# Unit 0 of a fused convolution and MLP: diagonal taps on turned blocks in place of band matmuls, and what goes with it

## The chip, the cores and the metric

One core of one Trainium2 chip. The time is that of one execution of the program on the device, in microseconds (us); the number that counts is the median of several runs. All times below are in us unless marked otherwise.

## The reference

`x` is (8, 4096, 192) in fp32, `weight` (8 heads, 7 taps), `w_in` (192, 2048), `w_out` (2048, 192). A causal convolution along the sequence with softmaxed taps, one set of taps for each group of 24 channels, is followed by a two-layer MLP:

```python
w = softmax(weight, axis=-1)                       # 8 x 7
out[b, s, h, g] = sum_k w[h, k] * x_pad[b, s + k, h, g]   # x_pad: 6 zero rows ahead of the sequence
h = out.reshape(32768, 192) @ w_in
y = (h * cos(h)) @ w_out                           # 32768 x 192, fp32
```

## The kernel before

**Tiles and units.** The 32768 tokens are cut into 64 tiles of 512 tokens; two tiles are a unit of 1024 tokens, eight blocks of 128. Each tile runs *product 1* (`mm1`, L488, matmul on L503): for each of 8 pairs of 128 hidden columns, h0 to h7, six matmuls with 64 contraction rows each, two of them side by side on the two halves of the PE array, write one `h` tile in PSUM, 128 x 1024 fp32. `gcu` (L506) then lets ACT write `cs = sin(h + pi/2)` (L510) and DVE `g = h * cs` (L514). *Product 2* (`mm2_step`, L523, matmul on L552) sums 64 steps of two matmuls into two PSUM banks `o_ps0` and `o_ps1`; `evac` (L567) copies them out and `store` writes them. `h` tiles come from a pool of three; the same pool serves the convolutions of later units, so a new tile waits until an old one has been read.

**Convolution of a unit.** `conv_part` (units 1 to 3) and `conv_unit` (from 4) multiply blocks of x, cast to bf16 on POOL (`cast_unit`, L207), with band matrices `band` (128 x 8 x 256) that hold the taps on diagonals; the result is copied by ACT to `ct`, doubled, and turned into channel-major form `cT` by a transposing DMA (`turn_unit`, L309). Product 1 reads `cT`.

**The start, which the change rebuilds.** `weight` is fetched as 4 rows of 14 numbers (L81). x of unit 0 is fetched in two halves: four blocks at once (L114), four more only after the SP queue has waited for `diag` (L406, L407); behind them stand unit 1 (L408 to L410) and, after another wait, `w_out` (L441 to L443). `w_in` is fetched in bf16 by two DMAs on POOL's queue (L111, L112, called on L165), behind the building of two small masks on POOL. PE runs 3 and 9 matmuls on zeros (`keep_warm`, L134) around one that spreads the taps over the partitions (L150); softmax of the taps in six small operations on DVE and ACT (L175 to L185); `prod` and `diag` (L401, L404) turn them into pieces of the band, which DVE, POOL and ACT copy to `band` in 16 pieces (L412 to L416). `conv_first` (L427) convolves four blocks with 32 matmuls of 48 columns, ACT and DVE copy them doubled to `ct` (L438), `turn_first` (L445) turns them with 12 matmuls against `ident` into PSUM, and ACT and DVE copy those to `cT` (L457). The other four blocks of unit 0 are convolved within tile 0 (`conv_rest`, L459, token `r`) and turned by a DMA (token `X0`).

**Order.** The schedule is manual: each engine does its instructions in the order in which the program writes them. For each tile two strings give that order. In the PE string `h3` is product 1 of pair 3 (`h0a`, `h0b` its halves), `m11` eleven steps of product 2, `d11`/`c11` the two band groups of unit 1, `w5` five matmuls on zeros, `W0`/`W1` POOL's cast of a half of `w_out`, `K1` POOL's cast of unit 1, `L2` the load of unit 2. In the ACT string `s3` is `gcu` of pair 3 and `er`, `ed11` copies of a convolution. For the first tile:

```python
PE_FIRST[0]  = "K1 h0a h0b W0 h1 h2 h3 r h4 w5 d11 w4 h5 d21 W1 c11 X0 m1 h6 m11 h7 L2 c21 D1"
ACT_FIRST[0] = "s0a s0b s1 s2 er s3 s4 ed11 ed21 s5 ec11 s6 ec21 s7"
```

Of the kernel before, what the change touches and what calls it, by code (L numbers as in the profile page):

```python
# [16 lines left out]
def kernel(  # L17
# [40 lines left out]

    xf = x.rearrange("b s d -> (b s) d")
# [20 lines left out]
    w_row = consts.tile([4, HQ * K], FP32)  # L80
    nc.scalar.dma_start(out=w_row, in_=weight.rearrange("(q h) k -> q (h k)", q=4))  # L81
# [25 lines left out]
    w = consts.tile([128, NC, NP, 128], BF16)  # L107
    w_src = moe_w_in.rearrange("(m k) (t f) -> t m k f", k=NC, t=2)
    HP = NP // 2
# [4 lines left out]
    load_unit(0, 0, NB)  # L114
# [12 lines left out]

    one = consts.tile([128, 1], FP32)
    nc.vector.memset(one, 1.0)
    zero = consts.tile([128, T], BF16)  # L130
    nc.vector.memset(zero, 0.0)  # L131
    idle = o_pools[0].tile([128, T], FP32, name="o_ps0")

    def keep_warm(n, bank=idle):  # L134
        for _ in range(n):
# [3 lines left out]
    quarter = consts.tile([4, 128], FP32)  # L139
    nc.gpsimd.memset(quarter, 1.0)  # L140
    nc.gpsimd.affine_select(out=quarter, in_=quarter, compare_op=ALU.is_ge, fill=0.0, base=0, pattern=[[1, 128]],
                            channel_multiplier=-32)
    nc.gpsimd.affine_select(out=quarter, in_=quarter, compare_op=ALU.is_ge, fill=0.0, base=31, pattern=[[-1, 128]],
                            channel_multiplier=32)
# [4 lines left out]
    w_bc = w_all[:, 0 : HQ * K].rearrange("p (h k) -> p h k", k=K)  # L149
    nc.tensor.matmul(out=w_all[:, 0 : HQ * K], lhsT=quarter, rhs=w_row, start=True, stop=True)  # L150
    keep_warm(9)


    xb0 = consts.tile([128, UB + 1, D], BF16, name="x_bf0")

    E = 32 + K - 1
    mask = consts.tile([128, E, K], BF16)
    nc.gpsimd.memset(mask[0:32], 0.0)
    nc.gpsimd.affine_select(out=mask[0:32], in_=mask[0:32], compare_op=ALU.not_equal, fill=1.0, base=1 - K,  # L159
                            pattern=[[1, E], [1, K]], channel_multiplier=-1)  # L160
    band = consts.tile([128, H, 256], BF16)
    nc.vector.memset(band, 0.0)
    for q, copy in enumerate((nc.vector.tensor_copy, nc.scalar.copy, nc.scalar.copy)):
        copy(out=mask[32 * q + 32 : 32 * q + 64], in_=mask[0:32])  # L164
    for t in range(2):  # L165
        load_w(t)
    nc.gpsimd.memset(xb0[:, 0, :], 0.0)
    ident = consts.tile([128, 128], BF16)
    nc.gpsimd.memset(ident, 0.0)
    nc.gpsimd.affine_select(out=ident, in_=ident, compare_op=ALU.not_equal, fill=1.0, base=0, pattern=[[1, 128]],  # L170
                            channel_multiplier=-1)
    wn = consts.tile([128, HQ, K], BF16)
    ct_bufs = [consts.tile([128, 2 * NC * NPB + 1, 64], BF16, name="ct_buf%d" % i) for i in range(2)]

    wmax = consts.tile([128, HQ, 1], FP32)  # L175
    nc.vector.tensor_reduce(out=wmax[:, :, 0], in_=w_bc, axis=mybir.AxisListType.X, op=ALU.max)
    wexp = consts.tile([128, HQ, K], FP32)
    nc.vector.tensor_tensor(out=wexp, in0=w_bc, in1=wmax.to_broadcast([128, HQ, K]), op=ALU.subtract)
    nc.scalar.activation(out=wexp, in_=wexp, func=AF.Exp)
    nc.scalar.activation(out=scrap, in_=one, func=AF.Sin)  # L180
    wsum = consts.tile([128, HQ, 1], FP32)
    nc.vector.tensor_reduce(out=wsum[:, :, 0], in_=wexp, axis=mybir.AxisListType.X, op=ALU.add)
    winv = consts.tile([128, HQ, 1], FP32)
    nc.vector.reciprocal(winv, wsum)
    nc.vector.tensor_tensor(out=wn, in0=wexp, in1=winv.to_broadcast([128, HQ, K]), op=ALU.mult)  # L185
    wo = consts.tile([128, NP, 2, D], BF16)
# [291 lines left out]

    conv_first()
    turn_first(0)  # L480
    turn_first(1)

# [241 lines left out]
```

## Time and profile before

| | |
|---|---|
| median of 3 runs | 705.23 (705.06 to 705.26) |
| the profiled execution | 705.18, its span 703.5 |
| busy over the span | PE 697.0, ACT 644.4, DVE 642.4, POOL 503.7 |
| the groups with most busy time | L514 DVE `g` 604.9, L510 ACT `cs` 511.0, L552 PE 420.6, L503 PE 407.0 |
| DMA | 100.09 MB, mean 142 GB/s |

How to read the profile: busy time is the time in which an engine runs an instruction. A row of a timeline gives start, duration, engine, line, operation, `out<-in` by the program's names, count, and in square brackets the idle time just before and what ended it. A row of a group gives busy time and mean length (ns) in place of the start. The chain of waits goes back from the last instruction, at each step to what released it. Matmul durations in a timeline hold some 0.17 of pipeline; neighbours in it start closer together than they are long. Times count from the start of the span; the kernel's first instruction on each engine stands at 0.8 to 0.9.

### The profile page before, as it was taken

How to read it: one execution, taken by the hardware profiler on the slowest of the kernel's cores; microseconds unless marked ns; L12 is line 12 of the kernel's file. 1: busy time of each engine (PE TensorE's matmuls, PEld its weight loads, DVE VectorE, ACT ScalarE, POOL GpSimd, SP SyncE). 2: the span in 40 equal slices, each digit the busy share in tenths (PEclk: the TensorE clock that was granted, in tenths of full speed). 3: DMA queues.
4: the chain of work that ended last, by engine and by line, in shares of the span. 5: the costliest groups of instructions: out<-in, count | busy, mean ns of one | idle time of the engine just before them, and what ended most of it. 6: DMA issues, size and time to landing. Idle time of an engine off the chain costs nothing.

```text
span 703.5 us, 26826 instructions
## 1 busy us (share of the span) xinstructions
PE 697.0 (99%) x11830; PEld 512.8 (73%) x11830; DVE 642.4 (91%) x598; ACT 644.4 (92%) x831; POOL 503.7 (72%) x214
## 2 busy tenths in 40 slices
PE   8999999999999999999999999999999999999997
PEld 4677777777777777777777777777777777777776
DVE  6889999999999999999999999999999999999996
ACT  7889999999999999999999999999999999999875
POOL 6524478977778877778877688877789778799400
PEclk9999999999999999999999999999999999999999
DMA  8964456667667768676656577577665576874331
GB/s 214 234 167 97 120 135 143 138 147 164 138 153 146 131 145 176 134 152 131 147 152 153 150 159 129 140 161 150 143 147 132 145 174 137 153 127 95 92 91 47
DMA packets 228292, 100.09 MB, mean 142 GB/s; under 512 B 156240, under 2 KB 227792, under 8 KB 228176
## 3 DMA queue, kind: packets, MB, share of 16 engines
q1 hardware_dynamic: 227464, 97.40, 62.7%
q8 instruction: 92, 1.51, 0.9%
q0 software_dynamic: 416, 0.79, 0.7%
q14 instruction: 24, 0.20, 0.1%
q10 hardware_dynamic: 296, 0.20, 0.1%
HBM read 31.36 MB, written 25.17 MB: 80 GB/s over the span
## 4 chain that ended last, share of the span: by engine, by line
PE 96%; DMA 1%; DVE 1%; POOL 0%; SPq 0%; ACT 0%; issue 0%; POOLq 0%
PE o_ps L552 48%; PE h L503 46%; PE h L277 2%; DMA wo_f<-in_moe_w_out_dram 1%; PE h L552 0%; SPq L124 0%; PE h L229 0%; DVE band L415 0%; POOL wo L120 0%; POOL mask L159 0%; DVE ct L438 0%; PE o_ps L432 0%; ACT mask L164 0%; DVE diag L404 0%; DVE prod L401 0%
## 5 line engine op out<-in xcount | busy, mean ns | idle before, releaser
L514 DVE TENSOR_TENSOR g<-h,cs 128x1024 bf16<-128x1024 f32 (+1 forms) x513 | 604.9, 1216 | 27.9 <-ACT cs L510 24.5
L510 ACT ACTIVATE cs<-h 128x1024 bf16<-128x1024 f32 (+1 forms) x513 | 511.0, 1021 | 44.0 <-PE h L503 30.6
L552 PEld LDWEIGHTS <-g 64*128 64x128 bf16 x8192 | 354.2, 94 | 102.2 <-issue 1.0
L552 PE MATMUL o_ps<-wo,g 64*128 64x192 bf16 x8128 | 420.6, 243 | 0.1
L503 PE MATMUL h<-cT,w 64*128 64x512 bf16 (+1 forms) x3078 | 407.0, 376 | 0.8 <-DVE g L514 0.4
L503 PEld LDWEIGHTS <-w 64*128 64x128 bf16 x3078 | 147.6, 94 | 75.0 <-issue 1.8
L211 POOL CAST xk<-x_f 128x768 bf16<-128x768 f32 (+1 forms) x56 | 76.4, 1367 | 113.9 <-DMA x_f<-in_x_dram 109.3
L363 POOL TENSOR_TENSOR raw_prod<-rT,tap 128x2784 f32<-128x2784 bf16 x28 | 135.3, 4832 | 0.2
L370 POOL TENSOR_TENSOR raw_prod<-raw_prod,pa 128x2088 f32<-128x2088 f32 x28 | 129.1, 4609 | 2.2
L356 ACT ACTIVATE pa<-rT,tap 128x348 f32<-128x348 bf16 x168 | 94.6, 580 | 0.0
L374 POOL TENSOR_TENSOR raw_prod<-raw_prod 128x1392 f32<-128x1392 f32 x28 | 87.9, 3138 | 2.2
L571 DVE COPY o_sb<-o_ps 128x384 f32<-128x384 f32 x62 | 34.6, 557 | 23.7 <-PE o_ps L552 23.5
L377 POOL TENSOR_TENSOR ro<-raw_prod 128x696 bf16<-128x696 f32 x28 | 46.5, 1660 | 2.2
L294 ACT CAST ct_buf<-h 112x480 bf16<-112x480 f32 x56 | 28.6, 562 | 4.1 <-PE h L277 0.6
L571 ACT COPY o_sb<-o_ps 128x384 f32<-128x384 f32 x64 | 30.8, 482 | 0.1
L277 PE MATMUL h<-xk,band 64*112 64x120 bf16 x448 | 21.2, 213 | 0.0
L277 PEld LDWEIGHTS <-band 64*112 64x112 bf16 x448 | 18.0, 127 | 0.0
L219 POOL CAST x_bf<-x_f 128x768 bf16<-128x768 f32 (+2 forms) x5 | 9.1, 1812 | 7.0 <-DMA x_f<-in_x_dram 6.9
L307 POOL COPY ct<-ct 128x1728 bf16<-128x1728 bf16 x3 | 4.9, 1630 | 8.9 <-ACT ct L239 8.9
L394 POOL COPY cT<-cT 128x144 bf16<-128x144 bf16 x3 | 0.9, 308 | 13.5 <-DMA cT<-ct 13.5
L136 PE MATMUL o_ps<-zero 128*128 128x512 bf16 x21 | 7.2, 492 | 1.3 <-DVE zero L131 1.3
L239 ACT CAST ct<-h 128x432 bf16<-128x432 f32 x12 | 5.9, 530 | 0.4 <-issue 0.4
(66 smaller groups left out, 52.7 us busy)
## 6 DMA issues: line engine op xcount, KB each, us to landing
out_dram<-o_sb SPq DMA_DIRECT2D x63, 384.0 KB, 3.7
x_f<-in_x_dram SPq DMA_DIRECT2D x28, 480.0 KB, 5.5
x_f<-in_x_dram SPq DMA_DIRECT2D x56, 192.0 KB, 2.7
cT<-ro SPq DMA_DIRECT2D x112, 87.0 KB, 2.3
x_f<-in_x_dram SPq DMA_DIRECT2D x4, 384.0 KB, 5.6
wo_f<-in_moe_w_out_dram SPq DMA_DIRECT2D x4, 384.0 KB, 7.9
x_f<-in_x_dram SPq DMA_DIRECT2D x2, 768.0 KB, 5.2
cT<-ct_buf SPq DMA_TRANSPOSE x56, 4.0
```

The source lines that it names most:

```text
L211: copy(out=xk[u][:, NC * n0 : NC * n1].rearrange("p (k n) m -> p k n m", k=NC), in_=x_tiles[u][:, n0:n1].rearrange("p n (m k) -> p k n m", ...
L277: return nc.tensor.matmul(out=ps[h // 4][0:OP, 0 : NPB * 4 * G].rearrange("p (m i r) -> p i m r", m=NC * NPB, i=4)[:, h % 4], lhsT=band[si ...
L356: mul(pa[u][:, j, part], tap_window(u, j)[:, part], tap[:, j : j + 1])
L363: nc.gpsimd.tensor_tensor(out=p, in0=tap_window(u, PA, K), in1=tap[:, PA:K].rearrange("p (j a b) -> p j a b", a=1, b=1).to_broadcast([128, ...
L370: add(out=p[:, 0:m], in0=p[:, 0:m], in1=a[:, done : done + m], op=ALU.add)
L374: add(out=p[:, 0:m], in0=p[:, 0:m], in1=p[:, n - m : n], op=ALU.add)
L377: add(out=ro[u], in0=p[:, 0], in1=p[:, 1], op=ALU.add)
L503: nc.tensor.matmul(out=h[:, i, n0 * 128 : n1 * 128], lhsT=w[rows, k, j, :], rhs=rhs, start=(k == 0), stop=(k == NC - 1))
L510: nc.scalar.activation(out=cs[:, :, part], in_=h[:, :, part], func=AF.Sin, bias=math.pi / 2.0, scale=1.0)
L514: nc.vector.tensor_tensor(out=g_tiles[t][:, 2 * j : 2 * j + 2, part], in0=h[:, :, part], in1=cs[:, :, part], op=ALU.mult)
L552: ms.append(nc.tensor.matmul(out=o_ps[tt, b, si], lhsT=g_tiles[tt][rows, f, s * 128 : (s + 1) * 128], rhs=wo[rows, f // 2, f % 2, :], star ...
L571: (copy or copies[b])(o_sb[t][:, 2 * b : 2 * b + 2, :].rearrange("p s d -> p (s d)"), o_ps.pop((t, b)))
```

## The change

Unit 0 is no longer convolved in token-major form with bands. Its blocks are cast to bf16 in an order in which the 64 numbers of a residue class of channels lie together (`cast_first`: blocks in pairs, by ACT, ACT, POOL, ACT), turned in pairs by matmuls against `ident` with the six tokens ahead of each block (`turn_pair`), copied to `xT`, and convolved there by 7 taps, each a matmul of 384 columns with a diagonal matrix `diag[:, j]` as weights and a shifted window of `xT`, for the two blocks of a pair side by side (`conv_pair`). The results are channel-major already and are copied to `cT` (`conv_copy`). Pairs 0 and 1 come ahead of tile 0; pairs 2 and 3 are the tokens `v2` and `v3` in it, in the place of `r` and `X0`; the matmuls on zeros `w5` and `w4` are gone from tile 0.

Beside that: `weight` is fetched as 8 rows of 7; softmax works on one row of 7 for each partition, with the sum taken by the exponential; x of unit 0 is fetched in three transfers (2, 2 and 4 blocks) with no wait between; unit 1 and `w_out` follow one wait on the SP queue, for DVE's copy of pair 0; `w_in` is asked for on POOL behind the building of `head`, `ident`, `pick` and `wide`; the 16 band pieces, now needed only from unit 1 on, are all copied by POOL; ahead of product 1 PE runs 3, 2, 1 and 3 matmuls on zeros. `tap` is copied from `wn` directly, `spread_taps` is gone. From tile 2 on the order strings are the same but for the marks `p` and `q`, which issue nothing.

```diff
-    w_row = consts.tile([4, HQ * K], FP32)
-    nc.scalar.dma_start(out=w_row, in_=weight.rearrange("(q h) k -> q (h k)", q=4))
+    w_row = consts.tile([H, K], FP32)
+    nc.scalar.dma_start(out=w_row, in_=weight)
-    load_unit(0, 0, NB)
+    load_unit(0, 0, NB // 2)
+    load_unit(0, NB // 2, NB)
+    load_unit(0, NB, UB)
+    head = consts.tile([H, 128], FP32)
+    nc.vector.memset(head, 0.0)
...
+    nc.vector.memset(ident, 0.0)
+    wide = consts.tile([128, E + K - 1], BF16)
+    nc.vector.memset(wide, 0.0)
+    xb0 = consts.tile([128, NC, UB + 1, 64], BF16, name="x_bf0")
+    nc.vector.memset(xb0[:, :, 0, :], 0.0)
+    nc.vector.memset(band, 0.0)
...
+    nc.gpsimd.affine_select(out=head, in_=head, compare_op=ALU.not_equal, fill=-1.0, base=0,
+                            pattern=[[0, 2], [-1, H], [0, R]], channel_multiplier=1)
+    nc.gpsimd.affine_select(out=ident, in_=ident, compare_op=ALU.not_equal, fill=1.0, base=0, pattern=[[1, 128]],
+                            channel_multiplier=-1)
+    pick = consts.tile([64, HQ, 128], BF16)
+    nc.gpsimd.tensor_copy(out=pick.rearrange("p i (q m) -> p i q m", q=4), in_=bass.AP(ident.tensor, ...))
+    for q in range(4):
+        nc.gpsimd.tensor_copy(out=wide[32 * q : 32 * q + 32, K - 1 : K + 31], in_=ident[32 * q : 32 * q + 32, 32 * q : 32 * q + 32])
+    for t in range(2):
+        load_w(t)
     nc.scalar.activation(out=scrap, in_=one, func=AF.Exp)
     keep_warm(3)
+    nc.tensor.matmul(out=w_bc, lhsT=head, rhs=w_row, start=True, stop=True)
+    keep_warm(2)
+    nc.vector.tensor_reduce(out=wmax, in_=w_bc, axis=mybir.AxisListType.X, op=ALU.min)
+    nc.scalar.activation(out=wexp, in_=w_bc, func=AF.Exp, bias=wmax, scale=-1.0, accum_out=wsum)
+    nc.vector.tensor_tensor(out=double, ...)
+    nc.vector.reciprocal(winv, wsum)
+    nc.vector.tensor_tensor(out=wn, in0=wexp, in1=winv.to_broadcast([128, K]), op=ALU.mult)
+    def turn_pair(p, ps):
+        to = ps[:, 0 : NC * (EDGE + 128)].rearrange("p (k t) -> p k t", k=NC)
+        for k in range(NC):
+            for prev, t0, t1 in ((0, EDGE, EDGE + 128), (1, 0, EDGE)):
+                n = 2 * p + 1 - prev
+                nc.tensor.matmul(out=to[:, k, t0:t1], lhsT=xb0[:, k, n : n + 2, :].rearrange("p n m -> p (n m)"),
+                                 rhs=ident[:, 128 - (t1 - t0) : 128], start=True, stop=True, skip_group_check=True)
+        return to
+    def conv_pair(p, ps, j0=0, j1=K):
+        for j in range(j0, j1):
+            for i in range(2):
+                rows = slice(64 * i, 64 * i + 64)
+                nc.tensor.matmul(out=ps[i][:, 0 : NC * 128].rearrange("p (k t) -> p k t", k=NC),
+                                 lhsT=diag[rows, j].rearrange("p t m -> p (t m)"), rhs=xT[rows, p, :, j : j + 128],
+                                 start=j == 0, stop=j == K - 1, skip_group_check=True)
+        return ps
+    def conv_copy(p, i, ps, copy):
+        m = NC * (2 * p + i)
+        return copy(out=cT[0][:, m * 128 : (m + NC) * 128], in_=ps[i][:, 0 : NC * 128])
+    def conv_later(p, cs):
+        ps = conv_pair(p, [o_bank(0), o_bank(1)])
+        yield
+        for i in range(2):
+            conv_copy(p, i, ps, copies[cs[i]])
...
+            yield
+    cast_first(0, 2, nc.scalar.copy)
...
+    to = [turn_pair(0, ring_banks()[0])]
+    keep_warm(1)
+    cast_first(2, 4, nc.scalar.copy)
+    to.append(turn_pair(1, ring_banks()[0]))
+    make_diag(0, 4)
+    nc.vector.tensor_copy(out=xT[:, 0], in_=to[0])
+    nc.scalar.activation(out=scrap, in_=one, func=AF.Sin)
+    cast_first(4, 6, nc.gpsimd.tensor_copy)
+    nc.scalar.copy(out=xT[:, 1], in_=to[1])
+    cast_first(6, 8, nc.scalar.copy)
+    make_diag(4, K)
...
+    ps0 = conv_pair(0, [o_bank(0), ring_banks()[0]])
+    conv_copy(0, 0, ps0, copies[0])
+    m = conv_copy(0, 1, ps0, copies[1])
+    rest = ring_banks()
+    to = [turn_pair(2 + i, rest[i]) for i in range(2)]
+    nc.scalar.copy(out=xT[:, 2:4], in_=...)
+    ps1 = conv_pair(1, [ring_banks()[0], o_bank(1)])
+    keep_warm(3, ring_banks()[0])
...
+    conv_copy(1, 0, ps1, copies[0])
+    conv_copy(1, 1, ps1, copies[1])
+    tc.add_manual_dep(nc.sync.nop().ins, m.ins.name, sync_dep, reason="order of the transfers")
     load_unit(1, 0, NB)
     load_unit(1, NB, UB)
     load_edges(1)
+    load_wo(0)
+    load_wo(1)
+    for i in range(16):
+        q, rows = divmod(i, 4)
+        nc.gpsimd.tensor_copy(out=band[...], in_=bands[32 * q : 32 * q + 32])
-    PE_FIRST = ["K1 h0a h0b W0 h1 h2 h3 r h4 w5 d11 w4 h5 d21 W1 c11 X0 m1 h6 m11 h7 L2 c21 D1",
+    PE_FIRST = ["K1 h0a h0b h1 v2 h2 h3 v3 W0 h4 d11 h5 d21 W1 c11 m1 h6 m11 h7 L2 c21 D1",
-    ACT_FIRST = ["s0a s0b s1 s2 er s3 s4 ed11 ed21 s5 ec11 s6 ec21 s7",
+    ACT_FIRST = ["s0a s0b s1 ev2 ev2 s2 s3 ev3 ev3 s4 ed11 ed21 s5 ec11 s6 ec21 s7",
```

In `copies` entry 0 is ACT, entry 1 DVE; `ev2 ev2` are the copies of pair 2's first block by ACT and of its second by DVE.

217 lines of the change are left out of this document (71 added, 146 removed), and 13 rows, old and new, of tables (ACT_FIRST, PE_FIRST).

## The prediction

> **What bounds the kernel now.** I read the page first, then the chain of waits in order of time, then the timelines of the first 40 us.
>
> ```profile
> 0.00:11.00 11.00, 8.79 (x67) 4.02 (x67) 7.28 (x21) 7.39 (x13) 6.20 (x21) 1.00 0.72 150
> ...
> 22.60:36.00 13.40, 13.36 (x208) 9.50 (x209) 11.24 (x11) 11.53 (x16) 8.22 (x5) 1.00 1.13 261
> ```
> Columns: stretch, length, busy time (instructions) of PE, PEld, DVE, ACT and POOL, granted clock, DMA, GB/s. From 22.6 us on PE is full (13.36 of 13.40) with work that the change leaves alone. So the change is worth exactly what it does to the moment at which PE becomes full: tile 1's first product 1, now at 22.81.
>
> ```profile
> 12.16 8.84 DMA wo_f<-in_moe_w_out_dram
> ...
> 21.12 1.48 POOL wo L120
> 22.64 0.34 PE o_ps L552 x4
> 22.98 0.65 PE h L503 x6
> ...
> 24.36 1.07 PE o_ps L552 x26
> ...
> 29.76 0.48 PE h L229 x4
> ```
> In the chain of waits that moment hangs on w_out: its last transfer lands at 21.0, POOL casts it until 22.6, PE goes on with product 2. (The last rows give prices: six matmuls of product 1 take 0.65, a step of product 2, two matmuls, 0.083, a band group 0.48.) Close behind stands a second chain, that of tile 0's products:
>
> ```profile
> 1.31 1.46 PE L136 MATMUL o_ps<-zero 128*128 128x512 bf16 x3 [1.31 <-DVE zero L131]
> ...
> 3.24 3.48 PE L136 MATMUL o_ps<-zero 128*128 128x512 bf16 x9
> ...
> 10.60 1.62 PE L503 MATMUL h<-cT,w 64*128 64x256 bf16 x18 [0.18 <-DVE cT L457]
> ...
> 15.46 1.25 PE L136 MATMUL o_ps<-zero 128*128 128x512 bf16 x5
> ...
> 17.05 1.02 PE L136 MATMUL o_ps<-zero 128*128 128x512 bf16 x4
> ...
> 18.21 0.82 PE L503 MATMUL h<-cT,w 64*128 64x512 bf16 x6
> ...
> 21.41 0.82 PE L503 MATMUL h<-cT,w 64*128 64x512 bf16 x6 [0.15 <-DVE g L514]
> ...
> 22.81 0.82 PE L503 MATMUL h<-cT,w 64*128 64x512 bf16 x6
> ...
> 35.44 0.81 PE L503 MATMUL h<-cT,w 64*128 64x512 bf16 x6
> ```
> ```profile
> 11.77 1.29 DVE L514 TENSOR_TENSOR g<-h,cs 128x512 bf16<-128x512 f32 x2 [0.75 <-ACT cs L510]
> 13.32 2.35 DVE L514 TENSOR_TENSOR g<-h,cs 128x1024 bf16<-128x1024 f32 x2 [0.26 <-ACT cs L510]
> 16.93 2.36 DVE L514 TENSOR_TENSOR g<-h,cs 128x1024 bf16<-128x1024 f32 x2 [1.26 <-ACT cs L510]
> 20.13 2.56 DVE L514 TENSOR_TENSOR g<-h,cs 128x1024 bf16<-128x1024 f32 x2 [0.84 <-ACT cs L510]
> ```
> ```profile
> 14.47 1.50 ACT L472 CAST ct<-o_ps 128x768 bf16<-128x768 f32 x2
> ...
> 17.68 0.97 ACT L239 CAST ct<-h 128x432 bf16<-128x432 f32 x2
> 19.07 1.02 ACT L510 ACTIVATE cs<-h 128x1024 bf16<-128x1024 f32 x1 [0.35 <-PE h L503]
> ```
> Three ring buffers hold product 1, so h5 (18.21) waits until DVE has done g3 (first of the pair at 16.93, over at 18.15), and h7 (21.41) until g5 (first of the pair at 20.13, over at 21.36). The chain is h0, g1, g3, h5, the sine of h5, g5, h7. The 9 matmuls on zeros at 15.46 and 17.05 stand only where PE waits anyway.
>
> **The change part by part.** *w_in.* Both kernels ask for it on POOL's queue; the new one only after six other operations.
>
> ```profile
> 2.98 1.43 POOL L112 DMA_DIRECT2D w<-in_moe_w_in_dram  x2
> ```
> ```profile
> L415 POOL CAST band<-diag 32x76 bf16<-32x76 f32 x7 | 1.7, 243 | 1.0 <-DVE diag L404 0.7
> L307 POOL COPY ct<-ct 128x1728 bf16<-128x1728 bf16 x1 | 1.6, 1631 | 0.0
> ...
> L170 POOL TENSOR_SCALAR_AFFINE_SELECT ident<-ident 128x128 bf16<-128x128 bf16 x1 | 0.5, 499 | 0.1
> ...
> L141 POOL TENSOR_SCALAR_AFFINE_SELECT quarter<-quarter 4x128 f32<-4x128 f32 x1 | 0.3, 283 | 0.1
> ```
> ```profile
> L112 POOL DMA_DIRECT2D w<-in_moe_w_in_dram x2: 632/718/804, 3.0 to 3.8; - x2
> ...
> DMA to landing us min/median/max: 5.5/6.0/6.6
> ```
> The second transfer is issued 0.80 behind the first, at 3.78, and lands 6.6 later, at 10.38, just ahead of the first product at 10.60. New: the select of head (0.28) can start at about 1.1, that of ident when DVE has zeroed it, about 1.6, and ends at 2.1. The copy of pick, 256 elements, is estimated from the rows of 76 and 1728 elements (0.24 and 1.63) at 0.40. Four copies of 32 elements at about 0.22, with gaps as between the band copies, take 1.0. So w is asked for at 3.5 instead of 2.98, **+0.52**, and lands at 10.9. Bounds: +0.3 (copies at 0.2, no gaps) to +1.7, if in addition x's other half, now ahead of it, takes 1.2 from it. That is 0.39 MB at the 320 GB/s of this row (1 us each from 0):
>
> ```profile
> GB/s 0 6 215 172 61 152 158 111 160 242 369 358 327 276 305 329 326 331 240 30 60 289 274 372 267 286 330 270 38 100 290 290 294 240 262 313 321 340 95 208
> ```
> The row speaks for no loss: the first half of x moved in slices 2 and 3, w begins only in slice 4; the other half fits in before about 4.8, and w's first bytes would now come at 5.0. I take +0.52.
>
> *Unit 0 ahead of that.* Removed: 32 band matmuls, 12 turns, the mask, four PSUM copies. Added: per pair of blocks 6 small turns, a copy to xT, 14 tap matmuls of 384 columns, two copies.
>
> ```profile
> L180 ACT ACT_TABLE_LOAD x1 | 1.3, 1283 | 0.0
> L219 ACT CAST x_bf<-x_f 128x768 bf16<-128x768 f32 x1 | 1.2, 1214 | 0.0
> ...
> L457 ACT CAST cT<-h 128x384 bf16<-128x384 f32 x2 | 1.0, 479 | 0.5 <-PE h L453 0.4
> ```
> ```profile
> L457 DVE CAST cT<-h 128x384 bf16<-128x384 f32 x1 | 0.6, 558 | 0.0
> ```
> ```profile
> 4.56 0.17 DVE L185 TENSOR_TENSOR wn<-wexp,winv 128x14 bf16<-128x14 f32 x1
> ```
> Tap matmuls use 64 rows each, two side by side as in product 1; at its rate (0.65 for three times 512 columns) a pair of blocks takes 7 x 0.163 = 1.14, at that of the band groups (0.48 for 864 columns) 1.5. I take 1.14, since the operands lie as in product 1. wn, now ready at 4.73, comes at about 4.2: a subtraction and a sum (0.2 each) fall away, and the exponential no longer stands behind ACT's mask copies. ACT casts two blocks by 4.5 and two by 5.2 (0.7 each, by 1.21 for four), loads the sine table until 6.5, copies xT (0.5) and casts the last two by 7.8. PE: turns until 6.4, taps of pair 0 until 7.55, turns of pairs 2 and 3 until 8.4, taps of pair 1 until 9.5, three zeros until 10.2; the last cT copies end at 10.2 too. So unit 0 is done 0.7 before w. **First product: 10.95 instead of 10.60**, and whatever the taps save at the head is hidden behind w.
>
> *Tile 0.* From 10.95 with the old distances: g0 at 12.12, g1 13.67 to 14.81 (two take 2.35, one 1.22, so the next starts after 1.13). Taps of pair 2 follow h1 on PE, 12.28 to 13.42. Their first copy (ACT, 0.48) ends at 14.1, in the place of the two of 1.50 now at 14.47; the sine of h2 runs 14.2 to 15.25. Their second copy is DVE's, behind g1: 14.81 to 15.37. Pair 3 needs that bank and waits for it (PE 15.4 to 16.54); h4 follows until 17.19. g2 starts at 15.35, g3 at 16.49 instead of 16.93 or later, done 17.7: **h5 at 17.73 instead of 18.21**. But ACT now has the sine of h4 only at 17.38, since h4 came behind pair 3; then come the two copies of unit 1 (0.97 in the row) and the sine of h5 at 19.15 instead of 19.07. So g5 at 20.2, **h7 at 21.43 instead of 21.41**: the gain has gone again.
>
> *w_out.* On SP's queue x1, w_out and then x2 now stand behind one wait, for the second copy of pair 0 (8.3); POOL's casts wait for them. 0.88 MB and 1.57 MB, from w's end at 10.3, at 320 GB/s: landed by about 18.6 instead of 21.0, as the unit 0 transpose is gone. POOL has 16 band copies (0.29 apart, 4.6, from 9.0 to 13.7), unit 1's two casts (2.7 to 2.8; to 16.4, as in this row), then w_out until about 20.1.
>
> ```profile
> 13.77 2.81 POOL L219 CAST x_bf<-x_f 128x768 bf16<-128x768 f32 x2
> ...
> 32.97 0.31 POOL L394 COPY cT<-cT 128x144 bf16<-128x144 bf16 x1 [0.41 <-DMA cT<-ct]
> ```
> Product 2 wants the second half at 22.4: the old last wait goes, cover 2 us. What is late next is h7 itself: its 0.65 and 6 steps of 0.083 end at 22.57.
>
> The sum: 22.57 - 22.81 = **-0.24**. Tile 2's first product (35.44 now) needs unit 1 mended, over at 33.28 in the second row; that gets no later, and 2.1 us cover it. The profiled execution took 705.18 around its span of 703.5; 704.94, and by the median of 705.23, 705.0: I say **704.9**. A measurement here tells about 0.2%, 1.4 us, from no change.
>
> [...]
>
> ```profile
> 1.31 0.61 PE L136 MATMUL o_ps<-zero 128*128 128x512 bf16 x1 [1.31 <-DVE zero L131]
> ```
> Zeros at 1.31 follow each other at 0.42 (1.46 for three, 0.61 for one), at 15.46 and 17.05 at 0.23 (1.25 for five, 1.02 for four): PE ran at half rate until some time within the nine at 3.24, though the granted clock column says 1.00. [...]
>
> **The rivals.**
> - *PE stays at half rate through the taps* (slower). Each PE term doubles: pair 0 until 8.65, turns until 9.95, pair 1 until 12.2, three zeros until 13.5. Product 1 then starts at 13.5, not 10.95: +2.55, **707.5**. It decides when the head passes w's 10.95, so one slow pair alone costs nothing. For it: 9 zeros fewer, waits for casts. Against: in my walk PE still works most of the time from 2.7 to 6.
> - *w lands late*, by x's half: 12.1 instead of 10.9, all behind it moves 1:1: **706.1**. For it: both now come together. Against: the GB/s row.
> - *The ring doesn't bind.* If ACT and DVE keep up better than my walk, PE alone sets the end: 10.95 and 8 products (5.4), two pairs (2.28), unit 1's two band groups (0.96), 18 steps (1.49) give 21.05, 1.76 earlier: **703.4**. For it: no zeros left to run. Against: today g3 ends as h5 starts and g5 as h7 starts.
>
> **How the numbers follow.** Forecast 0.55 (own range 704.2 to 705.9: w +0.3 to +0.9, tap matmuls at 1.5, ACT's order 0.3 either way); ring 0.15; late w 0.18, of which a third goes beyond 706.6 together with a slow pair; half rate 0.12. Faster by over 0.2%: 0.15; within: 0.55 + 0.12 = 0.67; slower: 0.12 + 0.06 = 0.18. The range goes from the ring's 703.4 to 706.8, which holds late w and leaves out the half rate.
>
> **What would show it.** Right: w issued near 3.5, PE idle or on zeros before the first L503 group near 11, that wait put down to w's DMA; no wait of w_out's cast for PE; DVE's copy of pair 2 just ahead of pair 3's taps; h7 near 21.4. Wrong: tap matmuls 0.32 apart after 7 us; a first product before 10.5; tile 1's first product before 21.8 or after 24.

## The result, and the profile after

The changed kernel takes 707.13 (median of 8 executions, 706.67 to 707.88) against 705.19 (8 executions, 705.04 to 705.28) for the one before: ratio 1.0028, 95% interval 1.0020 to 1.0037, slower by 1.9 us. The forecast was 704.9 with a range up to 706.8. The profiled execution took 706.75 with a span of 705.0, 1.5 longer than the span before. Its times fall into two groups, near 706.7 and near 707.5; those of the kernel before do not. What parts the two groups, no run shows.

The chain of waits, in order of time (start, length, what; its longest pieces), now begins with w's transfer, where w_out's stood before:

```profile
3.83 8.52 DMA w<-in_moe_w_in_dram
12.40 1.47 PE h L503 x17
16.76 2.35 DVE g L514 x2
```
The view of w's tile and POOL's timeline say when w was asked for and how long it took:

```profile
3.02 1.44 POOL L113 DMA_DIRECT2D w<-in_moe_w_in_dram  x2
```
```profile
L113 POOL DMA_DIRECT2D w<-in_moe_w_in_dram x2: 632/720/807, 3.0 to 3.8; - x2
...
DMA to landing us min/median/max: 7.2/7.9/8.5
```
POOL issues it at 3.02, 0.04 later than before. But the halves land 7.2 and 8.5 after their issue (5.5 and 6.6 before), the second at 12.35 instead of 10.38. PE's timeline from the taps to tile 1:

```profile
7.48 0.52 PE L419 MATMUL o_ps<-xT,diag 64*128 64x384 bf16 x1
...
7.80 0.52 PE L419 MATMUL o_ps<-xT,diag 64*128 64x384 bf16 x1
...
9.02 0.32 PE L419 MATMUL h<-xT,diag 64*128 64x384 bf16 x1
...
9.19 0.32 PE L419 MATMUL h<-xT,diag 64*128 64x384 bf16 x1
...
10.10 0.82 PE L152 MATMUL h<-zero 128*128 128x512 bf16 x2
10.86 0.28 PE L503 MATMUL h<-cT,w 64*128 64x256 bf16 x1
12.40 1.47 PE L503 MATMUL h<-cT,w 64*128 64x256 bf16 x17 [1.26 <-DMA w<-in_moe_w_in_dram]
```
```profile
13.61 1.42 PE L419 MATMUL o_ps<-xT,diag 64*128 64x384 bf16 x14
...
16.05 0.32 PE L419 MATMUL o_ps<-xT,diag 64*128 64x384 bf16 x1
16.71 1.30 PE L419 MATMUL o_ps<-xT,diag 64*128 64x384 bf16 x13 [0.34 <-DVE cT L426]
...
22.79 0.82 PE L503 MATMUL h<-cT,w 64*128 64x512 bf16 x6
23.93 0.83 PE L503 MATMUL h<-cT,w 64*128 64x512 bf16 x6
```
Unit 0's taps are over at 10.1, its last copy to `cT` at 10.80, and the first matmul that needs only w's first half runs at 10.86. The next one stands until w's second half is there, at 12.40. From then on everything follows at the distances of the forecast, and tile 1's first product begins at 23.93 instead of 22.81: +1.12. From there PE is full, as before (12.30 of 12.30 us in the first row below, which has the columns of the prediction's first fence). Of the 1.57 between the profiled executions 1.12 is there at 23.93. Product by product the two traces show that 0.08 more comes at 224 us and 0.24 at 587 us, and the rest at and behind the end; why, no run shows.

```profile
23.70:36.00 12.30, 12.30 (x196) 8.78 (x191) 10.98 (x11) 10.90 (x14) 6.86 (x5) 1.00 0.76 179
```

### The profile page after: what moved, and what is told of

Same layout as the page of the kernel before. It is cut to its first block, busy times and chain, and to the rows that moved or that the text cites. A ratio compares the mean times of both kernels' runs of the same rounds, so it can differ in the third digit from the quotient of the medians.

```text
span 705.0 us, 26829 instructions
## 1 busy us (share of the span) xinstructions
PE 697.5 (99%) x11834; PEld 514.8 (73%) x11835; DVE 642.5 (91%) x597; ACT 643.6 (91%) x830; POOL 503.8 (71%) x220
## 4 chain that ended last, share of the span: by engine, by line
PE 97%; DMA 1%; DVE 0%; POOL 0%; ACT 0%; issue 0%; POOLq 0%
PE o_ps L552 48%; PE h L503 47%; PE h L273 2%; DMA w<-in_moe_w_in_dram 1%; PE h L552 0%; PE h L229 0%; DVE g L514 0%; PE o_ps L419 0%; ACT cs L510 0%; ACT ct L239 0%; POOL wide L164 0%; POOL w L113 0%; DVE cT L426 0%; POOL head L155 0%; POOL pick L161 0%
## 5 line engine op out<-in xcount | busy, mean ns | idle before, releaser
L219 POOL CAST x_bf<-x_f 128x1728 bf16<-128x1728 f32 (+2 forms) x4 | 7.8, 1966 | 0.8 <-DMA x_f<-in_x_dram 0.7
L419 PE MATMUL o_ps<-xT,diag 64*128 64x384 bf16 x42 | 6.8, 356 | 0.3 <-DVE cT L426 0.3
L480 POOL CAST band<-bands 32x76 bf16<-32x76 f32 x16 | 3.9, 241 | 3.4 <-DVE bands L467 2.7
```

## Experiments

The question: why does w land 2 us late, when it was asked for at the same time? Each ratio is to runs of the kernel before on the same chip (medians 705.09 to 705.15). "Product 1" below is the first group that needs both halves of w; "zeros" are matmuls on zeros; `WARM` holds how many of them stand behind the softmax's matmul and how many between the turns of the first two pairs, (2, 1) in the changed kernel. "2+2+4" is x in transfers of two, two and four blocks, as the changed kernel asks for it.

**e1, no second half of x.** Half of unit 0's output is then that of other data.

```diff
-    load_unit(0, NB, UB)
-             in_=x_tiles[0][:, n0:n1, :].rearrange("p n (m k) -> p n k m", k=NC))
+             in_=x_tiles[0][:, n0 % NB : n0 % NB + n1 - n0, :].rearrange("p n (m k) -> p n k m", k=NC))
```


> The changed kernel without the transfer of the second half of x of unit 0: blocks 4 to 7 are computed from blocks 0 to 3, so half of unit 0's output is other data; all instructions but that one DMA stay. Theory X (x's second half, now ahead of w_in, holds some DMA engines and so w_in back): w_in's second transfer lands at about 10.5 instead of 12.35, the first product starts near 10.6 instead of 12.40, and the time falls by about 1.8, to 704.9 to 705.4. Rival Y (unit 1's transfers, issued from 8.4, cut into w_in's tail): w_in lands near 12 as before, time within 0.3 of 706.8. Rival H (the taps at half rate hold the head): time unchanged.

Measured: 705.57 (704.58 to 706.32), ratio 1.0003 (0.9994 to 1.0012). w's tile:

```profile
DMA to landing us min/median/max: 5.5/6.0/6.6
```
The landing of the kernel before is back: without x's second half w is not late. (Tile 1 began at 23.07 all the same; that comes up again at e16.)

**e2, w ahead of all else on POOL.**

```diff
+    for t in range(2):
+        load_w(t)
     nc.gpsimd.affine_select(out=head, in_=head, ...)
...
-    for t in range(2):
-        load_w(t)
     scrap = consts.tile([128, 1], FP32)
```


> The changed kernel with w_in asked for as POOL's first act, ahead of the four builds (about 2.1 earlier), x after it on its own queue as it was. Theory X: w_in's packets start near 2.5 and land at 9 to 10.5, while the second half of x comes later, at 7 to 10; the first product then starts when the taps of pair 1 are done, 10.2 to 11, time 704.5 to 705.7. Rival Y: no or little gain, w_in lands near 12 once more, 706.5 to 707. Rival H: head unchanged, 706.8.

Measured: 712.42 (711.58 to 712.82), ratio 1.0101 (1.0088 to 1.0115). All theories missed. Asked for at 1.3 and 2.1, w still lands only 8.6 and 10.5 later, and x comes so late that PE stands still for 5 us:

```profile
13.70 0.96 PE L411 MATMUL h<-ident,x_bf 128*128 128x128 bf16 x12 [4.99 <-POOL x_bf L397]
...
18.34 1.62 PE L503 MATMUL h<-cT,w 64*128 64x256 bf16 x18
```
**e3, unit 1's x asked for later**, to see whether its first packets hold up w's last ones.

```diff
-    conv_copy(1, 1, ps1, copies[1])
+    m = conv_copy(1, 1, ps1, copies[1])
     tc.add_manual_dep(nc.sync.nop().ins, m.ins.name, sync_dep, reason="order of the transfers")
```


> The changed kernel with the SP queue's wait put on the last copy to cT (10.8) instead of pair 0's (8.9), so that unit 1 and w_out are asked for 1.9 later. Theory X: w_in lands at 12.0 to 12.35 all the same, first product 12.1 to 12.4; the time is equal, or up to 0.5 longer if w_out's cast becomes the last wait. Rival Y: w_in's tail loses its competitor, lands at 10.8 to 11.2, first product near 11.1, time 1 us less, 705.5 to 706.

Measured: 706.86 (706.04 to 708.59), ratio 1.0028 (1.0018 to 1.0038). Unit 1's first packets start at 11.18 instead of 9.99, and w came no earlier (7.8 and 9.0 after issue): unit 1 is not the cause.

**e4, the kernel before with x whole at once**, in two transfers of four blocks.

```diff
     load_unit(0, 0, NB)
+    load_unit(0, NB, UB)
...
-    load_unit(0, NB, UB)
```


> The kernel before with one thing of the change: the second half of x of unit 0 is asked for at once behind the first, without the wait. Theory X: w_in lands at 11.8 to 12.4 instead of 10.4, the first product starts there instead of at 10.60, and tile 1's first product goes from 22.81 to 23.8 or later: 706.2 to 707.0. Rivals Y and H: w_in lands at 10.4 as before, and with x's second half there early the time is that of before or less, 704.7 to 705.3.

Measured: 705.15 (705.01 to 705.33), ratio 1.0000 (0.9991 to 1.0009), w 5.7 and 6.9 after issue. The same bytes ahead of w cost 0.3 there, not 2: the second half of x is not enough by itself, and my theory fell in its plain form. What differed between this run and the changed kernel, of x's transfers, was the cut: 4+4 blocks against 2+2+4.

**e5, the changed kernel with x in 4+4; e6, the kernel before with x in 2+2+4.**

```diff
-    load_unit(0, 0, NB // 2)
-    load_unit(0, NB // 2, NB)
+    load_unit(0, 0, NB)
```
```diff
-    load_unit(0, 0, NB)
+    load_unit(0, 0, NB // 2)
+    load_unit(0, NB // 2, NB)
+    load_unit(0, NB, UB)
...
-    load_unit(0, NB, UB)
```


> The changed kernel with unit 0's x in two transfers of four blocks where it has three of two, two and four; nothing else differs. Theory S (the cut in three makes the tail): w's second half lands about 10.7 us, as in the kernel before with x whole, where it took 6.9 us from its issue; product 1 follows unit 0, which starts some 0.5 us later since the first two blocks now land with the third and fourth; first product about 11.0, and since TensorE goes at half rate through pair 0, tile 1's first product about 22.9 against 23.93; about 705.4. Theory P (the tail comes from what VectorE and GpSimd do while w's transfer is written out): w lands at 12.3 as in the changed kernel, 707.0. A third, that any x whole ahead of w leaves a tail in this program for a reason not seen: like P.

> The kernel before, with all of unit 0's x asked for at once in three transfers of two, two and four blocks, as the changed kernel asks for it; unit 0 itself as before. Theory S: w lands about 12.3 instead of 10.7 (x in two transfers) and 10.38 (the kernel before), so the first product 1 at about 12.1 to 12.4, tile 1's first product +1 us, 706.3. Theory P: w lands at 10.7 and the time is that of the kernel before, 705.2.

Measured: e5 706.27 (705.53 to 706.9), ratio 1.0016 (1.0007 to 1.0025), w 5.7 and 7.1 after issue; e6 **708.88** (708.64 to 709.42), ratio 1.0054 (1.0041 to 1.0066). In e5 w is in time, and 1.1 of the 1.9 is still there, more than expected: unit 0 itself ends later, and in the profile product 1 begins at 11.26 and tile 1 at 23.38. In e6 the cut alone, put into the kernel before, costs 3.7 us, more than the whole change does. PE in e6, and a stretch behind it (the stretch's last three columns are granted clock, DMA share and GB/s):

```profile
11.42 0.28 PE L504 MATMUL h<-cT,w 64*128 64x256 bf16 x1 [0.98 <-DMA w<-in_moe_w_in_dram]
13.72 0.61 PE L504 MATMUL h<-cT,w 64*128 64x256 bf16 x4 [2.03 <-DMA w<-in_moe_w_in_dram]
```
```profile
13.70:17.00 3.30, 3.28 (x22) 2.23 (x24) 1.33 (x2) 1.70 (x3) 2.08 (x2) 0.50 1.11 313
```
Part of the 3.7 is the granted clock, 0.50 behind the two waits for w; the end of "Why the prediction was wrong" comes back to it. Where the cut shows is the DMA at 3.5 us. First e4, then e6, then the changed kernel:

```profile
3.50:4.00 0.50, 0.50 (x2) 0.15 (x1) 0.18 (x2) 0.48 (x2) 0.50 (x2) 1.00 1.10 370
4.00:4.50 0.50, 0.50 (x3) 0.17 (x2) 0.31 (x2) 0.48 (x2) 0.50 (x2) 1.00 1.10 370
```
```profile
3.50:4.00 0.50, 0.50 (x2) 0.15 (x1) 0.19 (x2) 0.48 (x2) 0.50 (x2) 1.00 0.64 112
4.00:4.50 0.50, 0.50 (x3) 0.16 (x2) 0.30 (x2) 0.48 (x2) 0.50 (x2) 1.00 1.00 326
```
```profile
3.50:4.00 0.50, 0.50 (x2) 0.00 (x0) 0.20 (x3) 0.44 (x3) 0.50 (x2) 1.00 0.74 157
4.00:4.50 0.50, 0.32 (x3) 0.07 (x2) 0.43 (x3) 0.50 (x2) 0.46 (x1) 1.00 0.91 266
```
Against 370 GB/s in e4 it moves 112 in e6 and 157 in the changed kernel: a hole, which I put down to the first two transfers, of two blocks each, running out before the third is under way. Behind it x's last packet starts at 5.22 in e6 and 5.52 in the changed kernel, against 4.93 in e4.

**e7, nine zeros ahead of product 1; e8, x in 4+4 with more zeros.**

```diff
-    keep_warm(3, ring_banks()[0])
+    keep_warm(9, ring_banks()[0])
```
```diff
-    WARM, OUT = (2, 1), ((0, 1), (0, 1))
+    WARM, OUT = (4, 1), ((0, 1), (0, 1))
-    load_unit(0, 0, NB // 2)
-    load_unit(0, NB // 2, NB)
+    load_unit(0, 0, NB)
-    keep_warm(3, ring_banks()[0])
+    keep_warm(5, ring_banks()[0])
```


> The changed kernel with nine matmuls on zeros ahead of product 1 where it has three: at full rate they fill TensorE from 10.1 to about 12.1 us, while it waits for w. Theory C (TensorE, idle while it waits for w, falls back to half rate in some executions, and that is the second cluster of its times near 707.5): all executions come near 706.7, and the trace shows product 1 at full rate from its first instruction. Rival (the two clusters come from w's landing, which differs between executions): two clusters stay, median 707.1.

> The changed kernel with x in two transfers of four blocks, two more matmuls on zeros behind the softmax's matmul (four where it has two) so that TensorE never stands still from 1.3 us on, and five ahead of product 1. If the cut in three and TensorE's half rate are the two costs: full rate from about 6 us on, the taps of pair 0 at 0.16 us a pair where they took 0.32, unit 0 done by 9.5, w by 10.7, first product 10.8, tile 1's first product by 22.5 against 22.81 before: about 704.9, at or just below the kernel before. If w's tail stays in spite of the two transfers: 706.7 as the changed kernel.

Measured: e7 707.43 (707.07 to 708.57), ratio 1.0034 (1.0021 to 1.0046): PE ran the zeros at full rate (eight of them in 2.12), and no execution came below 707.07, so theory C fell; product 1 waited for w again (9.1 after issue here). Whether w's landing also makes the two groups, as the rival says, isn't shown. e8 705.80 (705.48 to 706.41), ratio 1.0010 (1.0001 to 1.0019): w 6.6 after issue, but the five zeros held product 1 until 11.46, and full rate came only at about 7.9 (taps 0.32 apart up to 7.80, 0.16 from 8.02 on), not 6.

**e9, x in 2+6; e10, e8 with two zeros; e11, the kernel before with x in 4+2+2; e12, the third transfer on ScalarE's queue.**

```diff
-    load_unit(0, NB // 2, NB)
-    load_unit(0, NB, UB)
+    load_unit(0, NB // 2, UB)
```
(e9 also has `WARM = (3, 1)` and two zeros ahead of product 1.) e10 is e8 with `keep_warm(2, ...)` for `keep_warm(5, ...)`. e11 against the kernel before, and e12 against the changed one:

```diff
+    load_unit(0, NB, NB + NB // 2)
+    load_unit(0, NB + NB // 2, UB)
...
-    load_unit(0, NB, UB)
```
```diff
-    load_unit(0, NB, UB)
+    load_unit(0, NB, UB, nc.scalar)
```


> A version meant to keep what the changed kernel has early and lose the tail: x in two transfers of two and six blocks, three matmuls on zeros behind the softmax's matmul (two before) and two ahead of product 1 (three before). In all runs with x in three transfers the engines moved 112 to 161 GB/s between 3.5 and 4.0 us, where those with two moved 358 to 370: the first two transfers of two blocks had run out before the third was under way. Theory S1 (that hole sets the engines apart, and w pays for it): the six blocks keep the engines fed, no hole, w's second half at 10.7; unit 0 done by 10.2; first product 10.9, tile 1's first product 22.4; 704.9, like the kernel before. Theory S2 (a transfer of two blocks is spread unevenly by itself): a tail as before, w at 12, 706.7.

> The changed kernel with x in two transfers of four blocks, four matmuls on zeros behind the softmax's matmul and two ahead of product 1 where the run with five began product 1 at 11.46. w lands at about 10.4 as there, the copies of unit 0's second pair end near 10.95, so product 1 begins at 11.0 instead of 11.46: 705.4 if every 0.45 us there counts, 705.8 if the start of product 1 isn't what sets the time.

> The kernel before with x whole at once in three transfers, of four, two and two blocks (two, two and four gave 708.88 with w's first product waiting until 13.72; four and four gave 705.15). Theory S1 (the hole): the first two transfers hold six blocks, enough for the engines until the third is under way, so no hole and no tail: w at 10.7, 705.2. Theory S3 (three transfers ahead of w make the tail, whatever their order): w at 12 or later, 706 to 709.

> The changed kernel with the third of x's transfers (four blocks) asked for on ScalarE's queue, where it need not stand behind the first two on SyncE's. Theory S1: it is under way before the first two run out, no hole, w's second half at 10.7, product 1 at about 11.0, tile 1's first product 22.5 to 22.9: 704.9 to 705.4. Theory S3: still three transfers, so the tail stays: 706.7 or later. ScalarE's first work is due at 3.5 us, so that its own issue costs it nothing.

Measured: e9 706.66 (706.08 to 707.33), ratio 1.0022 (1.0013 to 1.0031); e10 **705.36** (704.74 to 706.53), ratio 1.0005 (0.9996 to 1.0013); e11 705.51 (705.06 to 708.23), ratio 1.0010 (1.0001 to 1.0018); e12 705.82 (704.88 to 706.9), ratio 1.0010 (1.0001 to 1.0018). e11 says that three transfers in another order cost 0.4 and not 3.7 (though one execution reached 708.2): their number alone isn't it. e9 lands w in time (7.0 after issue) although it has a hole as well, an earlier one (141 GB/s from 3.0 to 3.5 us); its product 1 starts only at 12.09, since its second pair of blocks waits for all six (PE 0.76 for their cast) and PE went at half rate until 10 (taps 0.32 apart up to 8.96, 0.17 from 10.30 on). So, by one profile, a hole with three quarters of x still behind it does no harm to w. In e12's profiled execution, of 705.0, w is back with one queue changed:

```profile
DMA to landing us min/median/max: 5.6/6.1/6.6
```
```profile
10.86 1.48 PE L503 MATMUL h<-cT,w 64*128 64x256 bf16 x18
...
22.40 0.83 PE L503 MATMUL h<-cT,w 64*128 64x512 bf16 x6
```
Tile 1 begins at 22.40, 0.41 ahead of the kernel before. But e12's other executions go up to 706.9.

**e13 to e15, PE's idle time ahead of the taps closed and opened.** Theory R: the spread of e12 (704.88 to 706.9) comes from the moment at which PE goes over to full rate. e13 is e12 with `WARM = (3, 1)` and two zeros ahead of product 1; e14 the changed kernel with `WARM = (3, 1)`; e15 is e12 with `WARM = (0, 0)`.

> The changed kernel with the third of x's transfers on ScalarE's queue, three matmuls on zeros behind the softmax's matmul (two before), which close TensorE's idle 0.17 us ahead of the spread of the taps, and two ahead of product 1 (three before). [...] Rival V (the spread comes from w's landing or from elsewhere): 705.0 to 706.9 as without the extra matmul, median 705.8.

> The changed kernel with three matmuls on zeros behind the softmax's matmul where it has two, and nothing else: x stays in three transfers on SyncE's queue, so w lands near 12.4. Theory R: unit 0 is always done before w, so that the second group of executions near 707.5 goes and 706.7 is left, spread under 0.6. Rival V: 707.1, two groups, 706.7 to 707.9.

> The changed kernel with the third of x's transfers on ScalarE's queue, without the two matmuls on zeros behind the softmax's matmul and the one between the turns of the first two pairs, so that TensorE stands still from 3.3 to 4.5 and from 4.9 to 5.4 us; three stay ahead of product 1. w lands at 10.4 as with them. Theory R: the move to full rate comes later in more executions (after 8.7 us), the taps of pair 1 go at half rate too, unit 0 ends up to 1.4 us later; median about 706.4, against 705.8 with those matmuls. Rival V: 705.8, since these matmuls compute nothing that is used.

Measured: e13 706.44 (704.9 to 707.76), ratio 1.0020 (1.0010 to 1.0029); e14 707.32 (706.52 to 707.75), ratio 1.0031 (1.0019 to 1.0042); e15 705.67 (705.04 to 707.11), ratio 1.0007 (0.9998 to 1.0016). Theory R fell: the one with most idle time has the lowest median of the three. The profile of e13 caught its latest execution, 707.76, and shows where the time goes:

```profile
DMA to landing us min/median/max: 7.4/8.0/8.6
```
```profile
10.48 0.28 PE L503 MATMUL h<-cT,w 64*128 64x256 bf16 x1 [0.52 <-DMA w<-in_moe_w_in_dram]
12.44 1.52 PE L503 MATMUL h<-cT,w 64*128 64x256 bf16 x17 [1.68 <-DMA w<-in_moe_w_in_dram]
15.78 2.24 PE L503 MATMUL h<-cT,w 64*128 64x512 bf16 x12
```
The order of transfers is that of e12, and w is as late as in the changed kernel. e15's profiled execution (706.53) has w late as well, 8.4 after issue. So with x on two queues w was in time in one profiled execution and late in two, and in 2+2+4 on one queue it was late in all five (the changed kernel, e3, e6, e7, e14). And there is no hole in e13 (nor in e15, with 323 GB/s here):

```profile
3.50:4.00 0.50, 0.50 (x2) 0.15 (x1) 0.21 (x3) 0.45 (x3) 0.50 (x2) 1.00 0.98 318
```
So the hole isn't needed for a late w, and by e9 it isn't enough.

What is late shows in single packets. Counting w's 384 packets in e13's trace by their start: 43 from 9.0 to 9.5, 21 in the next half, and then 6, 6, 6 and 5 in each half microsecond until 11.8. At 0.17 to 0.18 a packet, 6 in half a microsecond are about the work of two of the 16 engines in the profile's DMA share (an estimate: two engines at 0.175 a packet start 5.7), so that 14 would have been done by 10 and two 2 us behind. The trace also has small packets of 4 bytes, 16 for each transfer and mostly behind its others; that each ends one engine's share is my reading, and the trace doesn't name engines. For x's third transfer in e13 14 of them start by 4.62 and two at 5.11 and 5.17; for w's two halves 30 of 32 start by 10.09 and two at 11.82 and 11.98. In e12 the last ones start at 4.68 and 10.06: none is behind, with x or with w. That the two late with x belong to the engines of the two late with w is likely, but not shown. The last packet of x itself starts at 5.14 in e13 and at 4.64 in e12, that of w at 9.91 in e12.

Over all profiled kernels with x whole ahead of w: in seven (e4, e5, e8 to e12) x's last packet starts at 5.00 or earlier and w's last one between 9.91 and 10.62; in the other seven (the changed kernel, e3, e6, e7, e13, e14, e15) they start at 5.14 to 5.52 and at 11.62 to 12.91.

**e16 and e17, without x's second half, idle time closed and opened** (half of unit 0's output is that of other data): e1 with `WARM = (3, 1)` and `(0, 0)`. **e18**, a version meant to beat both (its edit in parts; beside them `WARM = (3, 1)`, two zeros ahead of product 1, and the old casts and turns of pairs 2 and 3 go):

```diff
-    load_unit(0, NB, UB)
...
-    make_diag(4, K)
+    m = make_diag(4, K)
+    tc.add_manual_dep(nc.sync.nop().ins, m.ins.name, sync_dep, reason="order of the transfers")
+    load_unit(0, NB, UB)
...
+    for p in (2, 3):
+        cast_first(2 * p, 2 * p + 2, nc.gpsimd.tensor_copy)
+    def turn_later():
+        for p in (2, 3):
+            nc.vector.tensor_copy(out=xT[:, p], in_=turn_pair(p, o_bank(p - 2)))
+        yield
-    PE_FIRST = ["K1 h0a h0b h1 v2 h2 h3 v3 W0 h4 d11 ...
+    PE_FIRST = ["K1 h0a h0b h1 h2 t2 h3 v2 W0 h4 v3 d11 ...
```


> The changed kernel without the transfer of x's second half (unit 0's blocks 4 to 7 are computed from blocks 0 to 3, so half of that unit's output is that of other data), and with three matmuls on zeros behind the softmax's matmul instead of two, which close TensorE's idle time ahead of the taps. w can have no tail here. Theory R (the moment of TensorE's full rate is what is left): the run without the extra matmul had 704.6 to 706.3, median 705.57, with the rate going up at 9.4 us in its profile; now it goes up by 8.2 at the latest, unit 0 done by 10.2, median 705.0, spread under 0.8. Rival T (only w's tail matters, the rate not): 705.5, as without it.

> As the run beside it without x's second half (half of unit 0's output is that of other data), but with no matmul on zeros between the softmax's matmul and the taps, so that TensorE stands still from 3.3 to 4.5 and from 4.9 to 5.4 us. Theory R: TensorE goes over to full rate after 8.7 us in all executions, unit 0 ends near 11 to 11.4 and product 1 begins at 11.3 to 11.8 in place of 10.9 to 11.3; median 706.0. Rival T: 705.5, the same as with them.

> A version meant to beat both kernels, with the whole computation: x's second half is asked for only when VectorE has written the diagonals (about 7 us), so that it runs behind w; its casts go to GpSimd behind the copies of the bands, its turns and taps (pairs 2 and 3) into tile 0 behind the fourth and fifth of its products 1; three matmuls on zeros behind the softmax's matmul, two ahead of product 1. w lands at 10.4 in every execution, product 1 begins at 10.6 to 11.0, tile 1's first product at 22.3 to 22.6 against 22.81; 704.8, spread under 0.8. If pairs 2 and 3 hold tile 0 up where they stand now, 705.5 or more.

Measured: e16 705.64 (704.6 to 705.95), ratio 1.0004 (0.9995 to 1.0013); e17 705.76 (704.83 to 706.19), ratio 1.0007 (0.9998 to 1.0016). Neither differs from e1's 705.57, so the idle time does not decide. The rate itself does cost where w is early, though. In e16 the taps went at half rate until 9.65, with no idle time of PE ahead of them:

```profile
4.79 0.56 PE L410 MATMUL h<-ident,x_bf 128*128 128x128 bf16 x6
...
8.01 0.52 PE L418 MATMUL o_ps<-xT,diag 64*128 64x384 bf16 x1
...
9.36 0.47 PE L418 MATMUL h<-xT,diag 64*128 64x384 bf16 x1
...
9.65 0.34 PE L418 MATMUL h<-xT,diag 64*128 64x384 bf16 x1
...
11.50 1.48 PE L502 MATMUL h<-cT,w 64*128 64x256 bf16 x18
...
23.05 0.83 PE L502 MATMUL h<-cT,w 64*128 64x512 bf16 x6
```
In e10's profile PE was at full rate before its first turns (the first group takes 0.40 there and 0.56 in e16):

```profile
5.23 0.40 PE L410 MATMUL h<-ident,x_bf 128*128 128x128 bf16 x6
```
```profile
10.47 1.54 PE L502 MATMUL h<-cT,w 64*128 64x256 bf16 x18
...
22.30 0.83 PE L502 MATMUL h<-cT,w 64*128 64x512 bf16 x6
```
Product 1 starts 1.03 earlier (one zero fewer, 0.2 of it), tile 1 0.75 earlier, and that execution took 704.86. This sets one profile beside one other, and x is asked for differently in the two. What sets the moment of full rate is not settled; PE was without idle time ahead of it in both. With `WARM = (3, 1)` it came near 6.9 in e13, 7.9 in e14 and 9.6 in e16, so e16's "by 8.2 at the latest" is not borne out; with `(0, 0)` it came near 9.6 in e15 and 9.8 in e17.

e18: 709.23 (707.33 to 709.3), ratio 1.0049 (1.0037 to 1.0062). w came in time and product 1 at 10.24, but the branch of its expectation that priced pairs 2 and 3 happened: their casts, put behind 16 band copies on POOL, came late and PE waited for them in the middle of tile 0; behind that wait the granted clock fell here too (six matmuls of product 1 take 1.46 at 16.25 and 0.81 at 19.30).

```profile
15.11 0.40 PE L410 MATMUL o_ps<-ident,x_bf 128*128 128x128 bf16 x6 [1.85 <-POOL x_bf L396]
```
No version beat the kernel before by more than can be measured; of those with the whole computation e4, e10 and e15 can't be told from it.

## Why the prediction was wrong

The step that failed is the landing of w. I had it asked for at 3.5 and landing at 10.9, "the row speaks for no loss"; it was asked for at 3.02 and landed at 12.35. Two errors of opposite sign:

- *The issue, +0.52: too much.* Measured +0.04. POOL's six small operations took the place of the mask's with almost nothing left over.
- *x's other half: "no loss", measured 1.9* (8.5 instead of 6.6 from issue to landing). I argued with bytes: at 320 GB/s the other half fits in before w's first packets. As bytes it nearly does: in two transfers x's last packet starts at 4.93, w's first at 4.58, and the cost is 0.3 (e4). But w landed behind its last packet, not when the bytes divided by the rate were through: in the changed kernel that packet starts at 11.64 and w has landed at 12.35, in the kernel before at 9.85 and 10.38. With the cut in three x's last packet starts later (5.52 against e4's 4.93), and in e13 two of the small packets came late with x and two later still with w. That the cut delays w is shown both ways: put into the kernel before it does (e6, 9.9 against e4's 6.9 from issue to landing), taken out of the changed one it doesn't (e5, 7.1 against 8.5). That lagging engines carry it is read from packets, not tested by itself; why 0.5 us behind with x became 2 us with w stays open. In the kernel before only half of x stood ahead of w, and the DMA ran empty in between:

```profile
3.50:4.00 0.50, 0.50 (x2) 0.15 (x1) 0.19 (x2) 0.48 (x2) 0.50 (x2) 1.00 0.08 25
4.00:4.50 0.50, 0.50 (x3) 0.16 (x2) 0.31 (x2) 0.48 (x2) 0.50 (x2) 1.00 0.00 0
```

In e13's trace each half of w has 16 packets of 4 bytes, and w counts as landed (8.6 after issue, at 12.4) only behind the last of them, at 11.98.

The other steps:

- *First product 10.95.* For w's first half it was 10.86. Unit 0 was done at 10.80, 0.6 later than the walk's 10.2 and just ahead of the 10.95, so that part of the walk held partly by luck: pair 0 went at half rate (0.32 apart, 7.48 to 7.80) and pair 1 at full rate (0.17 apart, 9.02 to 9.19).
- *Tile 0, 11.62 from first product to tile 1's.* Measured 11.53 (12.40 to 23.93). Pair 3 waiting for DVE's copy (0.34), h4 behind it, h7 1.14 ahead of tile 1's first product: all as walked. With w in time the forecast's gain appears: e12's profile has tile 1 at 22.40 (forecast 22.57) and 705.0.
- *w_out by 20.1, cover 2 us.* Too early by 2.3, since POOL waited for the transfers:

```profile
18.26 1.47 POOL L123 CAST wo<-wo_f 128x1536 bf16<-128x1536 f32 x1 [0.62 <-DMA wo_f<-in_moe_w_out_dram]
20.93 1.47 POOL L123 CAST wo<-wo_f 128x1536 bf16<-128x1536 f32 x1 [1.21 <-DMA wo_f<-in_moe_w_out_dram]
```
  The second cast ends at 22.40, where the forecast wanted that half; PE did not wait for it, with everything 1.1 later. With w in time, in e12's profile, it ends at 21.44: a cover of 1, not 2.
- *Rivals.* "w lands late, by x's half", at 12.1 and 706.1, is what happened (12.35; profiled execution 706.75, median 707.13), with its place right and its reason half right: not the bytes alone but the cut. The half rate was there in pair 0, hidden behind w, as its text allowed; the sign named for it (taps 0.32 apart after 7 us) appeared. That fewer zeros and waits for casts would keep PE slow was an estimate; no run shows what ends the half rate, and in the profiles it ended between 4.79 (e10) and 10.22 (e9), by the first record of the granted clock. The ring bound as forecast.
- *The chances.* Both rivals that made it slower were real, but I gave them 0.18 beyond the bound together; the spread between executions, 1.2 us, was not in the range at all.
- *Slips in the working that decided nothing.* With turns and all doubled, the half-rate walk ends at 13.9, not 13.5; w_out "by 18.6" follows from w's landing at 10.9, not from 10.3; the ring's terms add up to 21.08, not 21.05.

A late w is paid for twice in some executions. In e3 PE waited 0.63 and then 1.70 for w, and went at half rate afterwards, which the granted clock shows here (last row; same columns as above):

```profile
10.87 0.28 PE L503 MATMUL h<-cT,w 64*128 64x256 bf16 x1 [0.63 <-DMA w<-in_moe_w_in_dram]
12.85 1.60 PE L503 MATMUL h<-cT,w 64*128 64x256 bf16 x15 [1.70 <-DMA w<-in_moe_w_in_dram]
```
```profile
14.46 2.65 PE L419 MATMUL o_ps<-xT,diag 64*128 64x384 bf16 x14
```
```profile
13.70:17.00 3.30, 3.30 (x22) 2.52 (x20) 2.33 (x3) 1.85 (x4) 2.26 (x2) 0.50 1.03 289
```
14 taps take 2.65 where the changed kernel's took 1.42; that execution took 708.1. In e2 PE is slow as well behind its wait of 4.99 (taps 0.32 apart from 14.89 on); in e3 two waits of together 2.33, with a matmul between them, were enough.

The traces' clock records say more. In e3, e6, e13 and e18 the clock is halved for 3.41 us (13.63 to 17.04 in e3), in e2 for twice that. Counting PE's idle time in stretches of 3.41 us from the first record on, as far as about 20 us, the clock fell behind those with 1.84 (e13), 2.29 (e18), 2.33 (e3), 2.87 (e6) and 3.14 us (e2) of idle time, and behind none with 1.70 (e14) or less. Each halved stretch lowers the mean granted clock of an execution by 0.0024 (an estimate: half of 3.41 over 706.3), to 0.998; in the profiles without one the mean is 0.999 or more. 0.998 or less is on record for all five executions of e6 and all four of e2, three of five of e18, two of e3's eight and of e13's nine, one of e14's six and of e11's twelve (the 708.2), and for none of the changed kernel's eight: its 1.9 holds no fall of the clock, e6's 3.7 does.

## What to carry to other kernels

Ask what stands ahead of a transfer in the DMA engines, not only when it is issued: bytes over bandwidth gave 0, the trace 1.9 us. Here w was late in all five profiled executions with 2+2+4 on one queue, in two of three with the third transfer on another queue, and in none of four with 4+4: the large transfer first was the safe cut. Look at when the last packets start, not only at GB/s. A wait can also cost PE its rate afterwards: behind the waits for w of e3 (0.63 and 1.70) and e6 (0.98 and 2.03) the granted clock was 0.50, behind the one of 1.91 in e14 it was not. And where a step makes executions differ, one profile is one draw: e12's profile (705.0) and e13's (707.8) came from the same order of transfers.

## What the runs showed that I had not expected

- The same bytes of x ahead of w delay its second half by 0.3 in 4+4 (6.9 from issue to landing, 6.6 without them), 1.0 in 4+2+2 (7.6) and 3.3 in 2+2+4 (9.9), all in the kernel before.
- Asking for w 1.7 us earlier put tile 1's first product at 30.02, 6.1 later than in the changed kernel (e2): with w ahead, x came late, and x was the one that PE needed first.
- The granted clock reads 1.00 from 2 to 12 us in the changed kernel, while matmul distances of 0.32 and 0.17 tell half and full rate. The trace's records of the granted clock begin only where the distances change: at 8.30 there, 6.03 in the kernel before, 4.79 in e10, 9.68 in e16. Ahead of the first record the column's 1.00 stands for no record, not for full rate. Over all profiles they begin between 4.79 and 10.22 (e9).
- e8's profiled execution took 706.39 with a span of 703.8, 0.8 more outside the span than the other profiles; no row shows where.
